# The low half of the attention weights moved from GpSimd to VectorE, and more tiles for the rows of x2

## The chip, the cores and the metric

The kernel runs on one core of a Trainium2 chip. The metric is device time in microseconds, the median of several executions. The engines are TensorE (PE, with its weight loads shown as PEld), VectorE (DVE), ScalarE (ACT), GpSimd (POOL) and SyncE (SP, which issues DMAs). Each engine takes its instructions strictly in the order in which they were written for it, and waits on semaphores for the other engines and for DMAs.

## The reference

Three stages follow one another: windowed attention with four sink keys, a dense layer with a maximum over three products, and an expert layer in which every token is assigned to one of eight experts under a capacity.

```python
def _attn_ref(q, k, v, n_sink, window):            # 4 x 8 heads, 768 x 64
    scores = scale * np.matmul(q, k.transpose(0, 1, 3, 2))
    keep = is_sink | in_window                      # 4 sinks, window 128
    scores = np.where(keep, scores, -1000000000.0)
    scores = scores - np.max(scores, axis=-1, keepdims=True)
    a = np.exp(scores)
    a = a / (np.sum(a, axis=-1, keepdims=True) + 1e-09)
    return np.matmul(a, v).astype(np.float32)

def _moe_ref(x, w1, w2, w3, w_out):                 # 3072 x 512, 768 wide
    h = np.maximum(np.maximum(x @ w1, x @ w2), x @ w3)
    return (h @ w_out).astype(np.float32)

def _moe2_ref(x, w_gate, w1, w2):                   # 8 experts, 384 tokens each
    logits = x @ w_gate
    ...                                             # tokens to experts, best first, cap 384
    for e in range(E):
        mask = assigned == e
        h = np.maximum(x[mask] @ w1[e], 0.0)
        out[mask] = h @ w2[e]
    return out.astype(np.float32)
```

## The kernel before, in words

Products that must be exact enough for the routing are computed with split operands: a value x is written as a high part (x rounded to the matmul's format, made by ScalarE) and a low part (x minus the high part, a subtraction), and three products (high-high, high-low, low-high) stand for one.

**Attention** works on 32 pairs of heads over half a sequence each, four pairs to a group, eight groups. For one pair, `load` fetches the operands, `prep` splits keys, queries and values (lines 101 to 116), `score` computes the masked scores, `soft` the softmax (its last multiplication, line 154, is GpSimd's), and `pv` multiplies with the values. In `pv`, for each of the two heads, TensorE transposes the weights (line 25), VectorE masks them into the tile A (line 170, 128x768), ScalarE makes the high part H (line 184), GpSimd the low part L (line 185), and TensorE multiplies H and L with the values (line 189, into po). ScalarE and VectorE then join the halves (lines 191, 192). Ten of the 32 pairs are taken without a split ("native", the first eight and two more); the remaining 22 pairs run lines 184 and 185 twice each, 44 in all.

**The dense layer** takes a group's four tiles x (split on line 28 and 29) and, for each of six row blocks f, makes three products into two alternating banks mm (line 290), takes their maximum (line 292 on ScalarE, 293 on VectorE, tile hm), and splits it (lines 298 and 299, tile HL). `x2` multiplies HL with the output weights (line 315), three row tiles t of two halves u; ScalarE copies each half from the bank to a row tile (line 317, `xo` or `xq`) and a DMA writes the row tile to the array x2d in DRAM (line 326). Group 0 is written to DRAM and multiplied later; groups 5 and 6 are multiplied later too, by `by_rows` and by `x2` with the pool `hp` (rows `xq`), together with group 7. `load_out` and `logits` use `xo` as well.

**The expert layer** ranks the tokens (VectorE with small TensorE counts, class `Route`), gathers the rows of x2d, and runs eight experts whose weights are streamed and split (lines 557 to 563).

All of attention and the dense layer stands in one block whose order is set by a planner when the program is built (`tc.block(schedule_with_timeline_sim=True)`): the attention of the next group is woven between the matmuls of the present one. Tiles of a pool are reused in turn (`bufs`); a reuse waits for the last reader of the buffer, a DMA included.

Of the kernel before, what the change touches and what calls it, by code (L numbers as in the profile page):

```python
# [19 lines left out]
FT=mybir.dt.float32; FR=mybir.dt.float32r; BF=mybir.dt.bfloat16; I32=mybir.dt.int32; U8=mybir.dt.uint8; U32=mybir.dt.uint32  # L20
AF=mybir.ActivationFunctionType; OP=mybir.AluOpType; AX=mybir.AxisListType
NEG=-8.0e9
def f32(ap): return ap.bitcast(FT)
def flip(nc,out,x,ident):
    nc.tensor.transpose(out,x,f32(ident))  # L25

def split(nc,hl,x):
    nc.scalar.activation(hl[0],x,AF.Copy)
    nc.vector.tensor_tensor(hl[1],x,f32(hl[0]),op=OP.subtract)

class Attn:
# [123 lines left out]
    def pv(s,u,x):  # L155
        nc=s.nc; w=s.w; T=u['T'].rearrange('p u j -> p (u j)'); hf=u['hf']; nb=u['nb']; nat=u['nat']
        psk=s.pst.tile([128,512],FT,name="pt")
        for i in range(3): flip(nc,psk[:,i*128:(i+1)*128],T[:,264*i+128:264*i+256],s.ident)
        PB=s.pb[u['n']%2]
        nc.scalar.activation(PB[0:8],psk[0:8,:384],AF.Copy)  # L160
        nc.vector.tensor_tensor(PB[32:40],psk[0:8,:384],f32(PB[0:8]),op=OP.subtract)
        jobs=[]
        if hf: jobs.append((0,128,0,0))
        for i in range(3): jobs.append((i*256+128,256 if i<2 else 128,i*128,i+hf))
        for h in range(2):
            pt=s.psp.tile([128,512],FT,name="pp")
            for i in range(3):
                flip(nc,pt[:,i*128:(i+1)*128],T[:,i*264+136*h:i*264+136*h+128],s.ident)
            A=s.two(dict(n=u['n']*2+h),[128,3,2,128],FT,"A")
            nc.vector.tensor_tensor(A,pt[:,:384].rearrange("p (i q) -> p i q",q=128)[:,:,None,:].to_broadcast([128,3,2,128]),  # L170
                s.ul[:,None,:,:].to_broadcast([128,3,2,128]),op=OP.mult)
            Af=A.rearrange("p i u q -> p (i u q)")
            a=slice(64*h,64*h+64); o=slice(64-64*h,128-64*h)
            if nat:
                if h==0:
                    po=s.psv.tile([128,512],FT,name="po")
                    for a_ in range(2): nc.tensor.matmul(po[:,:384],u['VK'][:,a_,:],PB,start=(a_==0),stop=False,skip_group_check=True)
                for c,n,q,blk in jobs:
                    nc.tensor.matmul(po[a,q:q+n],u['vn'][:,blk,h,:],Af[:,c:c+n],start=False,stop=True,skip_group_check=True)  # L179
                if h==1:  # L180
                    for c in x: split(nc,c,po[:,:384]) if type(c) is tuple else nc.scalar.activation(c,po[:,:384],AF.Copy)
                continue
            H=w.tile([128,768],FR,name="H"); L=w.tile([128,768],FR,name="L")
            nc.scalar.activation(H,Af,AF.Copy)  # L184
            nc.gpsimd.tensor_tensor(L,Af,f32(H),op=OP.subtract)  # L185
            po=s.psv.tile([128,512],FT,name="po")
            for part in (H,L):
                for j,(c,n,q,blk) in enumerate(jobs):
                    nc.tensor.matmul(po[:,q:q+n],u['VS'][:,blk,128*h:128*h+128],part[:,c:c+n],start=(part is H and j==0),stop=False,skip_group_check=True)  # L189
            nc.tensor.matmul(po[:,:384],u['VK'][:,h,:],PB,start=False,stop=True,skip_group_check=True)  # L190
            nc.scalar.activation(x[0][a,:],po[o,:384],AF.Copy)
            nc.vector.tensor_tensor(x[0][a,:],po[a,:384],x[0][a,:],op=OP.add)
# [18 lines left out]
class Moe1:  # L211
    def __init__(s, tc, words,wgate, consts, wpool, main, conv, mm, pt, pss, ident):
        s.tc=tc; s.nc=tc.nc; s.mm=mm; s.pss=pss; s.main=main; s.conv=conv; s.ident=ident; s.consts=consts
        s.src=words; s.wgate=wgate
        s.W=[[wpool.tile([128,4,768],FR,name=f"w{i}{x}") for x in "hl"] for i in range(3)]
        s.WO=None; s.at=None; s.stage=None; s.HL=None; s.n=0; s.loads=[]
        s.WG=main.tile([128,6,16],FR,name="wgt")
    def split(s,src,hi,lo):
        nc=s.nc
# [19 lines left out]
        return R.bitcast(FT)  # L239
    def pair(s,p):  # L240
        return tuple(s.main.tile([128,384],FR,name=f"x{x}{p}",bufs=1) for x in "hl")
    def part(s,x,f):
        return s.HL[:,"hl".index(x)*6+f]
    def load_w(s,f):
# [59 lines left out]
    def x2(s,H,t0,LG,x2d,n=260,pool=None,keep=None):  # L304

        nc=s.nc; main=s.main
        for t in range(3):
            o=pool.tile([128,512],FT,name="xq",bufs=3) if pool else main.tile([128,520],FT,name="xo",bufs=1)
            for u in range(2):
                c=slice(0,260) if n==260 else slice(4-4*u,260-4*u)  # L310
                ps=s.mm.tile([128,512],FT,name="mm")
                k=0
                for f in range(6):
                    for a,b in ((0,0),(0,1),(1,0)):
                        nc.tensor.matmul(ps[:,:n],H[f][a][:,t*128:(t+1)*128],s.WO[b][:,f,u,c],start=(k==0),stop=(k==17)); k+=1  # L315
                with s.tc.high_priority():
                    nc.scalar.activation(o[:,u*n:(u+1)*n],ps[:,0:n],AF.Copy)
                    if keep is not None:
                        for d in (2*u,2*u+1):
                            h,l=keep(t,d); c=ps[:,(d-2*u)*128:(d-2*u)*128+128]  # L320
                            nc.scalar.activation(h,c,AF.Copy)
                            nc.vector.tensor_tensor(l,c,f32(h),op=OP.subtract)
            if n==260:
                o,e=s.row(o,0)
                nc.scalar.activation(LG[:,t0+t,:].rearrange("p (u e) -> p u e",u=2),e,AF.Copy)
            nc.scalar.dma_start(x2d[(t0+t)*128:(t0+t+1)*128,:],o)
# [10 lines left out]
    def by_rows(s,spill,t0,x2d,accs,pool):  # L337

        nc=s.nc
        ps=[accs.tile([128,512],FT,name=f"acc{t}") for t in range(3)]  # L340
        for f in range(6):
            H=tuple(s.main.tile([128,384],FR,name=f"x{x}{f%4}",bufs=1) for x in "hl")
            for d,x in zip(spill[f],H): nc.sync.dma_start(f32(x),d)
            for t in range(3):
                for j,(a,b) in enumerate(((0,0),(0,1),(1,0))):
                    nc.tensor.matmul(ps[t],H[a][:,t*128:(t+1)*128],s.row(s.WO[b],f*520)[0],start=(f+j==0),stop=(f==5 and j==2))
        for t in range(3):
            o=pool.tile([128,512],FT,name="xq",bufs=3)
            with s.tc.high_priority(): nc.scalar.activation(o,ps[t],AF.Copy)
            nc.scalar.dma_start(x2d[(t0+t)*128:(t0+t+1)*128,:],o)  # L350
    def logits(s,H,t0,LG):
# [15 lines left out]
class Route:  # L367
# [4 lines left out]
    M=128  # L372
# [175 lines left out]
class Moe2:  # L548

    def __init__(s,tc,w1,w2,x2d,out,wpool,act,main,mm,acc,pt,ident,nring,part):  # L550
        s.tc=tc; s.nc=tc.nc; s.w1=w1; s.w2=w2; s.x2d=x2d; s.out=out
        s.wp=wpool; s.act=act; s.main=main; s.ng=0; s.mm=mm; s.acc=acc; s.pt=pt; s.ident=ident; s.nring=nring; s.part=part
        s.scat=[]; s.n=-1
# [80 lines left out]
def attention_mixtures(tc,q,k,v,vs,words,wg,u1,u2,out,off=60,spread=(0,1,3,4),native=8,order='a0 a0 a0 a0 w a1 w a1 w a1 w a1 w w a2',order1='a2 o o o o o o a2 a2',back=1,at=(1,0),s1=300,s2=400,nring=6):  # L634
    nc=tc.nc
    PS=bass.MemoryType.PSUM
    with ExitStack() as ctx:
        P=lambda n,b,**kw: ctx.enter_context(tc.tile_pool(name=n,bufs=b,**kw))
        A_=lambda n,b,**kw: tc.alloc_tile_pool(name=n,bufs=b,**kw)
# [5 lines left out]
        A=Attn(tc,q,k,v,vs,consts,ac,pst,psp,pss,psv,work)  # L645
        M=Moe1(tc,words,wg,consts,wpool,main,conv,mm,pst,pss,A.ident)
# [3 lines left out]
        def att(g,p):  # L650
            xs.setdefault(g,[])
            u=A.load(g//2,g%2,p,4*g+p<native or 4*g+p in (10,11)); A.prep(u); A.score(u); A.soft(u)
            x=main.tile([128,384],FT,name=f"x{p}") if g else M.pair(p)
            A.pv(u,[x]); xs[g].append(x)
        def lw(f): M.load_w(f)
        def lo(f): M.load_out(f)
        with tc.block(schedule_with_timeline_sim=True):
# [3 lines left out]
            def emit(o,p):  # L661
                n=cnt[o]=cnt.get(o,-1)+1
                if o[0]=='a':
                    if p:
                        with tc.high_priority(offset=off): att(int(o[1:]),n)
                    else: att(int(o[1:]),n)
                elif o=='w': lw(n)
                else:
                    A.extra=None; lo(n)
                    if n==5:  # L670
                        conv.release()
                        A.extra=A_("extra",1,side="right"); A.no=('A',)
                        A.ql.append(A.zeros([A.extra.tile([128,384],FR,name=f'ql{h}b') for h in range(2)]))
            for o in order.split():
                if o=='a2': A.behind=M.loads[-1]
# [2 lines left out]
            for g in range(NG):  # L678
# [15 lines left out]
                H6,H=H if g==NG-1 else None,M.group(xs[g],sp if g==0 else sp2 if g==NG-3 else None,hp if g==NG-1 else None,rest,between)  # L694
# [107 lines left out]
```

## Time and profile before

| what | us |
|---|---|
| median of 3 runs | 985.83 (981.25 to 990.14) |
| the profiled execution | 981.21 |
| its span, first to last instruction | 979.4 |
| TensorE busy in the span | 936.7 |
| VectorE busy | 693.3 |
| ScalarE busy | 486.2 |
| GpSimd busy | 340.9 |

The profiled execution stands at the low end of the runs. A busy share is an average over stages: attention with the dense layer takes up roughly the first 600 us, the routing and the experts the rest. A kernel line in a row (L185) is the line of the listing above. "Granted clock" is the share of TensorE's full clock (1.00 is 2.4 GHz, 0.50 is 1.2 GHz).

### The profile page before, as it was taken

The page shows a single profiled execution, that of the slowest core. Times are in us where ns is not written, and L with a number is a line of the kernel's source. Part 1 is how long each engine was busy: PE and PEld are TensorE (multiplying, and loading weights), DVE is VectorE, ACT ScalarE, POOL GpSimd, SP SyncE. Part 2 cuts the span into 40 slices and gives each one's busy share as a digit, 9 for nine tenths or more (in the row PEclk, how much of TensorE's full clock was granted, in tenths as well). Part 3 has the DMA queues.
Part 4 walks back from the last instruction along what each step waited for, and adds up shares of the span by engine and source line. Part 5 has one row for each costly group of instructions (what it writes and reads, how often), then busy time and mean ns, then how long its engine had stood idle before and what let it go on. Part 6 is the DMA issues. An engine that isn't in the chain of part 4 may idle for free.

```text
span 979.4 us, 18512 instructions
## 1 busy us (share of the span) xinstructions
PE 936.7 (96%) x6552; PEld 855.7 (87%) x6552; DVE 693.3 (71%) x1811; ACT 486.2 (50%) x1341; POOL 340.9 (35%) x315
## 2 busy tenths in 40 slices
PE   6899999999999999989999999999999999999996
PEld 4578899889999999979999898798888888888895
DVE  6778877687888877795655445889989879873320
ACT  4477553777576766666653211233433434344431
POOL 3687556136434634434343000011203122053331
PEclk8999999999999999999999999999999999999999
DMA  7464322341123122122110002634345353454420
GB/s 209 134 223 157 109 65 69 108 137 47 49 78 86 40 70 66 55 66 77 58 60 1 1 1 87 205 125 130 124 136 173 93 166 101 159 200 146 136 79 32
DMA packets 54444, 99.36 MB, mean 101 GB/s; under 512 B 7792, under 2 KB 24688, under 8 KB 54352
## 3 DMA queue, kind: packets, MB, share of 16 engines
q1 hardware_dynamic: 44464, 75.90, 25.3%
q0 software_dynamic: 3840, 12.45, 3.6%
q10 hardware_dynamic: 6048, 9.83, 2.7%
q8 instruction: 51, 0.84, 0.4%
q14 instruction: 41, 0.34, 0.1%
HBM read 82.17 MB, written 16.12 MB: 100 GB/s over the span
## 4 chain that ended last, share of the span: by engine, by line
PE 75%; DVE 9%; issue 5%; DMA 5%; ACT 4%; POOL 1%; SPq 1%; POOLq 0%; DVEq 0%; ACTq 0%
PE mm L290 27%; PE mm L618 11%; PE acc L611 11%; PE mm L315 7%; PE po L189 3%; PE rc L416 2%; PE po L179 2%; PE ps L130 2%; PE pt L25 2%; PE pp L25 2%; DMA sa<-in_u_dram 1%; DMA qf<-in_q_dram 1%; PE ps L132 1%; PE ps L133 1%; PE po L190 1%
## 5 line engine op out<-in xcount | busy, mean ns | idle before, releaser
L611 PE MATMUL acc<-wbh,HL 128*128 128x512 f32 x384 | 131.7, 399 | 0.0
L185 POOL TENSOR_TENSOR L<-A_w,H 128x768 fp32r<-128x768 f32 x42 | 80.2, 1909 | 100.7 <-ACT H L184 99.8
L630 POOL DMA_INDIRECT out_dram<-og,idx x24 | 32.2, 1344 | 182.4 <-ACT og L629 179.1
L315 PE MATMUL mm<-woh,HL 128*128 128x260 f32 (+1 forms) x432 | 91.9, 302 | 3.6 <-DVE HL L299 2.2
L293 DVE TENSOR_TENSOR hm<-mm,hm 128x384 f32<-128x384 f32 x96 | 53.2, 554 | 56.0 <-PE mm L290 47.8
L562 ACT ACTIVATE wah<-sa 128x512 fp32r<-128x512 f32 x64 | 40.5, 632 | 92.2 <-PE mm L618 73.0
L611 PEld LDWEIGHTS acc<-wbh,HL 128*128 128x128 f32 x384 | 71.9, 189 | 12.8
L315 PEld LDWEIGHTS mm<-woh,HL 128*128 128x128 f32 x432 | 73.1, 200 | 7.0 <-DVE HL L299 2.9
L562 ACT ACTIVATE wbh<-sb 128x512 fp32r<-128x512 f32 x64 | 40.4, 632 | 74.6 <-PE acc L611 71.9
L611 PE MATMUL acc<-wbl,HL 128*128 128x512 f32 x192 | 77.2, 402 | 0.0
L618 PE MATMUL mm<-HL,wah 128*128 128x384 f32 x256 | 68.8, 344 | 0.0
L290 PE MATMUL mm<-xh,w0h 128*128 128x384 f32 x192 | 66.7, 347 | 1.2 <-DVE hm L293 1.0
L290 PE MATMUL mm<-xh,w1h 128*128 128x384 f32 x192 | 66.2, 345 | 1.5 <-ACT hm L292 0.7
L290 PE MATMUL mm<-xh,w2h 128*128 128x384 f32 x192 | 66.6, 347 | 0.0
L563 DVE TENSOR_TENSOR wbl<-sb,wbh 128x512 fp32r<-128x512 f32 x64 | 43.9, 687 | 31.7 <-ACT wbh L562 31.7
L290 PE MATMUL mm<-xh,w0l 128*128 128x384 f32 x192 | 64.9, 338 | 0.4 <-POOL w0l L221 0.4
L290 PE MATMUL mm<-xl,w0h 128*128 128x384 f32 x192 | 64.9, 338 | 0.1
L290 PE MATMUL mm<-xh,w1l 128*128 128x384 f32 x192 | 64.9, 338 | 0.0
L290 PE MATMUL mm<-xl,w2h 128*128 128x384 f32 x192 | 64.9, 338 | 0.0
L290 PE MATMUL mm<-xh,w2l 128*128 128x384 f32 x192 | 64.8, 338 | 0.0
L290 PE MATMUL mm<-xl,w1h 128*128 128x384 f32 x192 | 64.6, 337 | 0.0
L622 DVE SCALAR_TENSOR_TENSOR HL<-mm,HL 128x384 fp32r<-128x384 f32 x64 | 35.4, 554 | 40.8 <-ACT HL L621 40.6
(331 smaller groups left out, 2843.9 us busy)
## 6 DMA issues: line engine op xcount, KB each, us to landing
sa<-in_u_dram SPq DMA_DIRECT2D x64, 256.0 KB
sb<-in_u_dram SPq DMA_DIRECT2D x64, 256.0 KB
HL<-in_words_dram SPq DMA_DIRECT2D x18, 512.0 KB
qn<-in_q_dram SPq DMA_DIRECT2D x88, 96.0 KB
x2d<-xo ACTq DMA_DIRECT2D x15, 256.0 KB
kn<-in_k_dram SPq DMA_DIRECT2D x12, 264.0 KB
st<-in_words_dram SPq DMA_DIRECT2D x6, 512.0 KB
vn<-in_v_dram SPq DMA_DIRECT2D x12, 256.0 KB
```

The costliest lines, as they stand in the source:

```text
L25: nc.tensor.transpose(out,x,f32(ident))
L185: nc.gpsimd.tensor_tensor(L,Af,f32(H),op=OP.subtract)
L189: nc.tensor.matmul(po[:,q:q+n],u['VS'][:,blk,128*h:128*h+128],part[:,c:c+n],start=(part is H and j==0),stop=False,skip_group_check=True)
L290: nc.tensor.matmul(ps[:,:384],s.W[i][a][:,p,f*128:(f+1)*128],X[p][b],start=(n==0),stop=(n==11)); n+=1
L293: else: nc.vector.tensor_tensor(m,ps[:,:384],m,op=OP.max)
L315: nc.tensor.matmul(ps[:,:n],H[f][a][:,t*128:(t+1)*128],s.WO[b][:,f,u,c],start=(k==0),stop=(k==17)); k+=1
L562: nc.scalar.activation(h,src,AF.Copy)
L563: (nc.gpsimd if s.n>=6 and nm=="wa" else nc.vector).tensor_tensor(l,src,f32(h),op=OP.subtract)
L611: s.mms.append(nc.tensor.matmul(acc[t],H[f][a][:,t*128:(t+1)*128],W[f][1][b],start=(f==0 and n==0),stop=(f==F-1 and n==2))); n+=1
L618: s.mms.append(nc.tensor.matmul(ps[:,:384],W[f][0][a][:,k,:],X[k][b],start=(n==0),stop=(n==11))); n+=1
L622: nc.vector.scalar_tensor_tensor(l,ps[:,:384],0.0,f32(h),op0=OP.max,op1=OP.subtract)
L630: st=nc.gpsimd.indirect_dma_start(out=s.out,out_offset=bass.IndirectOffsetOnAxis(ap=idx[:,t:t+1],axis=0),in_=o,in_offset=None)
```

## The change

The subtraction that makes L moves from GpSimd to VectorE (line 185 in both). `x2` takes its row tiles `xo` in turn from the pool `main` and from a second pool, `extra`, in which a tile of the same name and size is laid out; the row tiles `xq` have four buffers instead of three. The planner is run again on the new program. Lines after 241 move down by 3.

```diff
-            nc.gpsimd.tensor_tensor(L,Af,f32(H),op=OP.subtract)
+            nc.vector.tensor_tensor(L,Af,f32(H),op=OP.subtract)
...
-        s.WO=None; s.at=None; s.stage=None; s.HL=None; s.n=0; s.loads=[]
+        s.WO=None; s.at=None; s.stage=None; s.HL=None; s.nx=0; s.second=None; s.n=0; s.loads=[]
...
+    def room(s,t):
+        s.nx+=1
+        return s.main if s.nx%2 else s.second
...
-            o=pool.tile([128,512],FT,name="xq",bufs=3) if pool else main.tile([128,520],FT,name="xo",bufs=1)
+            o=pool.tile([128,512],FT,name="xq",bufs=4) if pool else s.room(t).tile([128,520],FT,name="xo",bufs=1)
...
-            o=pool.tile([128,512],FT,name="xq",bufs=3)
+            o=pool.tile([128,512],FT,name="xq",bufs=4)
...
-                        A.extra=A_("extra",1,side="right"); A.no=('A',)
+                        A.extra=M.second=A_("extra",1,side="right"); A.no=('A',)
```

On VectorE, the end of the dense layer of group 3: from the last maximum of the group (writes hm, L293) to the low part of its last block (writes HL, L299), which the first row tile of `x2` needs. Before:

```order
614 L293 TENSOR_TENSOR hm<-mm,hm 128x384
615 L29 TENSOR_TENSOR xl_5076<-x_4616,xh_5075 128x384
616 L192 TENSOR_TENSOR x_5158<-po,x_5158 64x384
617 L170 TENSOR_TENSOR A_w<-pp,ul 128x768
618 L29 TENSOR_TENSOR xl_5080<-x_4785,xh_5079 128x384
619 L104 TENSOR_TENSOR ql0b<-qn_6055,qs_6067 64x384
620 L142 COPY_PREDICATED T_w<-ca,ps 128x128
621 L102 TENSOR_TENSOR kh_x<-kn,kh_x 64x528
622 L104 TENSOR_TENSOR ql1b<-qn_6056,qs_6068 64x384
623 L142 COPY_PREDICATED T_w<-ca,ps 128x128
624 L102 TENSOR_TENSOR kh_x<-kn,kh_x 64x528
625 L299 TENSOR_TENSOR HL<-hm,HL 128x384
```

The same place on VectorE with the change (L296 is the old L293, L302 the old L299):

```order
664 L296 TENSOR_TENSOR hm<-mm,hm 128x384
665 L29 TENSOR_TENSOR xl_5076<-x_4616,xh_5075 128x384
666 L29 TENSOR_TENSOR xl_5080<-x_4785,xh_5079 128x384
667 L142 COPY_PREDICATED T_w<-ca,ps 128x128 x2
668 L192 TENSOR_TENSOR x_5158<-po,x_5158 64x384
669 L302 TENSOR_TENSOR HL<-hm,HL 128x384
```

Ten operations stood between the two; now five do. The splits of the next pair's queries and keys (L104, L102) have moved ahead of the last maximum.

On GpSimd, two pairs of the same stretch, before (T is the softmax tile, vk and vsp the split values):

```order
158 L154 TENSOR_TENSOR T_x<-T_x,l 128x792
159 L185 TENSOR_TENSOR L<-A_w,H 128x768
160 L108 CAST vk_103<-vns 40x2x64
161 L116 TENSOR_TENSOR vsp<-vn,vsp 128x4x128
162 L109 TENSOR_TENSOR vk_103<-vns,vk_103 40x128
163 L185 TENSOR_TENSOR L<-A_w,H 128x768
164 L154 TENSOR_TENSOR T_w<-T_w,l 128x792
165 L185 TENSOR_TENSOR L<-A_w,H 128x768
```

GpSimd's queue with the change, two pairs:

```order
133 L154 TENSOR_TENSOR T_x<-T_x,l 128x792
134 L108 CAST vk_103<-vns 40x2x64
135 L109 TENSOR_TENSOR vk_103<-vns,vk_103 40x128
136 L116 TENSOR_TENSOR vsp<-vn,vsp 128x3x128
137 L154 TENSOR_TENSOR T_w<-T_w,l 128x792 x2
```

The subtractions are gone from between the others; what is left in GpSimd's queue is one line 154, 108, 109 and 116 to a pair, and a memset in some.

## Rows read from the trace of the kernel before

**Rows 1.** The page, part 1: busy us, share of the span, instructions.

```profile
PE 936.7 (96%) x6552; PEld 855.7 (87%) x6552; DVE 693.3 (71%) x1811; ACT 486.2 (50%) x1341; POOL 340.9 (35%) x315
```

**Rows 2.** By stage: stretch, length, busy us of each engine, granted clock, DMA share, GB/s.

```profile
130.00:545.00 415.00, 403.04 (x2675) 390.72 (x2674) 302.12 (x580) 257.97 (x789) 180.48 (x156) 0.98 0.21 64
275.00:290.00 15.00, 13.45 (x94) 12.62 (x93) 13.62 (x28) 10.25 (x39) 3.96 (x4) 0.89 0.28 83
350.00:365.00 15.00, 13.29 (x94) 12.74 (x93) 11.49 (x22) 11.80 (x38) 6.11 (x6) 0.89 0.21 65
420.00:445.00 25.00, 20.32 (x131) 19.25 (x129) 19.69 (x34) 15.98 (x54) 8.96 (x7) 0.86 0.15 49
```

**Rows 3.** Timeline, 430 to 437 us: start, length, engine, line; in brackets idle before.

```profile
431.33 1.81 POOL L185 TENSOR_TENSOR L<-A_w,H 128x768 fp32r<-128x768 f32 x1
433.52 0.98 POOL L116 TENSOR_TENSOR vsp<-vn,vsp 128x384 fp32r<-128x384 f32 x1
...
431.25 3.67 DVE L104 TENSOR_TENSOR ql1b<-qn,qs 64x384 fp32r<-64x384 f32 x1
...
435.40 0.36 PE L132 MATMUL ps<-kh_w,qs 128*128 128x260 f32 x1 [3.80 <-DVE T_w L142]
...
436.63 0.80 PE L315 MATMUL mm<-woh,HL 128*128 128x260 f32 x2 [0.76 <-DVE HL L299]
```

**Rows 4.** Timeline around 272 to 282 and 350 to 360 us.

```profile
272.94 1.86 POOL L185 TENSOR_TENSOR L<-A_w,H 128x768 fp32r<-128x768 f32 x1 [3.30 <-ACT H L184]
273.08 2.15 DVE L102 TENSOR_TENSOR kh_x<-kn,kh_x 64x396 fp32r<-64x396 f32 x1
...
279.96 0.51 PE L315 MATMUL mm<-woh,HL 128*128 128x260 f32 x2 [0.56 <-DVE HL L299]
...
282.02 0.36 PE L132 MATMUL ps<-kh_x,qs 128*128 128x260 f32 x1 [0.84 <-DVE T_w L137]
...
350.62 1.86 POOL L185 TENSOR_TENSOR L<-A_w,H 128x768 fp32r<-128x768 f32 x1 [6.82 <-ACT H L184]
...
350.93 1.97 DVE L104 TENSOR_TENSOR ql<-qn,qs 64x384 fp32r<-64x384 f32 x1
...
358.02 0.51 PE L315 MATMUL mm<-woh,HL 128*128 128x260 f32 x2 [0.91 <-DVE HL L299]
359.32 0.67 PE L189 MATMUL po<-H,vsp 128*128 128x128 f32 x4 [0.80 <-DVE x L192]
```

**Rows 5.** Groups by line, 130 to 545 us: busy us, mean ns, idle before.

```profile
L185 POOL TENSOR_TENSOR L<-A_w,H 128x768 fp32r<-128x768 f32 x42 | 80.2, 1909 | 100.7 <-ACT H L184 99.8 <-PE pp L25 0.6
...
L170 DVE TENSOR_TENSOR A_w<-pp,ul 128x768 f32<-128x768 f32 x45 | 42.8, 951 | 9.8 <-PE pp L25 7.5 <-POOL L L185 2.0
...
L102 DVE TENSOR_TENSOR kh_x<-kn,kh_x 64x528 fp32r<-64x528 f32 (+1 forms) x20 | 20.8, 1041 | 3.0 <-ACT kh_x L101 2.3
...
L104 DVE TENSOR_TENSOR ql<-qn,qs 64x384 fp32r<-64x384 f32 x19 | 18.2, 958 | 1.2 <-ACT qs L103 0.9
...
L104 DVE TENSOR_TENSOR ql1b<-qn,qs 64x384 fp32r<-64x384 f32 x10 | 11.6, 1159 | 0.7 <-PE ps L133 0.4
```

**Rows 6.** Lines 104 and 102, whole run: count, shortest/median/longest ns.

```profile
L104 DVE TENSOR_TENSOR ql<-qn,qs x24: 542/556/2197, 101.1 to 450.0; 64x384 fp32r<-64x384 f32 x24
...
L102 DVE TENSOR_TENSOR kh_x<-kn,kh_x x20: 565/702/2594, 184.1 to 474.9; 64x528 fp32r<-64x528 f32 x12, 64x396 fp32r<-64x396 f32 x8
```

**Rows 7.** Waits, 130 to 545 us: who for whom, us in total, times, longest.

```profile
ACT xo L317 <- DMA x2d<-xo: 2.1, 1, 2.1
```

**Rows 8.** Timeline, 630 to 638 us, row tiles of the last groups.

```profile
630.90 0.33 ACTq L350 DMA_DIRECT2D x2d<-xq  x1
...
635.58 0.38 ACT L317 ACTIVATE xq<-mm 128x256 f32<-128x256 f32 x1 [3.22 <-DMA x2d<-xq]
...
637.63 0.58 PE L315 MATMUL mm<-woh,hh 128*128 128x256 f32 x1 [2.35 <-DVE HL L322]
```

**Rows 9.** The stretch 635 to 641 us, columns as in Rows 2.

```profile
635.00:641.00 6.00, 3.65 (x20) 3.44 (x19) 4.81 (x17) 4.54 (x12) 2.23 (x2) 0.72 0.58 168
```

## The prediction, made before the changed kernel was timed

> **What bounds the kernel now.** I began with the busy shares of the page [rows 1]. TensorE is busy for 936.7 of a span of 979.4 us, so only what makes it stop or run slowly can be won; 43 us of idle time is all there is, and much of it lies in the start and in the expert layer, which the change does not touch. Next I read the table by stage [rows 2]. The first line is the stretch in which the moved subtraction runs: 415 us long, TensorE busy 403.0. The reader should see two things in it: 12.0 us idle, and a granted clock of 0.98. The three short lines show where the clock goes: 0.89, 0.89 and 0.86 over 15, 15 and 25 us. Half speed (1.2 GHz) was granted for a few microseconds in each, right after TensorE had stood still several times. What that costs is (1 - 0.89) x 15 twice, 1.65 each, and 0.14 x 25 = 3.5, together 6.8 us of work. So TensorE loses 12.0 + 6.8 = **18.8 us** in this stage. That is the most the stage can give.
>
> Then the timeline at the largest stop, at 435 us [rows 3]. VectorE's subtraction of line 104 takes 3.67 us; such an operation takes 0.556 us in the median [rows 6]. It begins at 431.25. GpSimd's line 185 begins at 431.33, line 116 follows behind a short operation and ends at 434.50, and VectorE's ends at 434.92. An operation of VectorE that reads two tiles of SBUF is held up as long as GpSimd is in an unbroken run. TensorE waits 3.80 us for the copy queued behind it on VectorE and 0.76 us for HL. The same happens at 273 us and at 351 us [rows 4]: line 102 takes 2.15 us beside line 185 (shorter form undisturbed 0.565, [rows 6]), line 104 takes 1.97 us beside line 185, and some microseconds later, once VectorE's queue has become late, TensorE waits 0.56, 0.84, 0.91 and 0.80 us. In those two cases the link runs through a queue that was continuously busy, not through one wait. The six waits come to 7.7 us, and all three losses of clock lie there. Of the stage's 18.8 us, **14.5 us** hang on holds by line 185.
>
> The Trainium skill (SBUF — State Buffer, section "Who interferes with whom") says that a VectorE instruction with two SBUF inputs contends with a GpSimd instruction that reads SBUF, and that the second to issue blocks until the first finishes. The trace agrees on the blocking, but here the hold lasted through three GpSimd operations, not one.
>
> **The change, part by part.** *Line 185 leaves GpSimd.* 42 of its 44 operations take 80.2 us [rows 5], nearly half of the 180.5 us in which GpSimd is busy in the stage [rows 2]. How much VectorE is held: lines 104 and 102, 49 operations in three groups [rows 5], take 18.2 + 11.6 + 20.8 = 50.6 us, and undisturbed 29 x 0.556 + 20 x 0.702 at most = 30.2 us [rows 6]. So 20.4 us are holds, 0.42 us for each operation. With 47% of the holding work gone, about 9.6 us of these holds go.
>
> *It comes to VectorE.* 44 operations on 128x768. The nearest row is line 170, same shape and type, 0.951 us [rows 5]: 44 x 0.951 = 41.8 us. It reads one input from PSUM; the new one reads two from SBUF, so the undisturbed 0.556 us for half as many elements bounds it at 1.11 us from above. Being of the kind that is held, each also gets what is left of the holds, 0.42 x 0.53 = 0.22 us, 9.8 us together. VectorE's busy time in the stage goes from 302 to about 302 + 41.8 + 9.8 - 9.6 = 344 us of 415, from 73 to 83%. This lies beside TensorE's matmuls and costs nothing as such; the cover is that VectorE still idles 17% of the time. If it were gone, every microsecond of VectorE would be one of TensorE. Behind the new operation in VectorE's queue stands mostly the addition of line 192 or a maximum of line 293, and TensorE waits for those.
>
> *The order is written anew.* On VectorE the stretch that cost most now has five operations instead of ten between the last maximum and HL, with lines 104 and 102 ahead of it; a hold there is shorter and hits less. GpSimd's queue keeps lines 154, 108, 109 and 116, now side by side, so its unbroken runs without line 185 go on. Loads on SP's queue shift among themselves; none of TensorE's waits in rows 3 and 4 ends on a load, so they cost nothing.
>
> Together: of the 14.5 us I take two thirds as won, **9.7 us**, because about half of the holds stay and the queue is fuller. Bounds: all 18.8 us won; or as much again lost, 18.8 us, if the added 42 us makes as many new stops as the holds did.
>
> *A second tile for xo.* ScalarE waits for a row tile's DMA once, 2.1 us [rows 7], and a second bank of mm hides that from TensorE. Nothing; if the cover goes, 2.1 us.
>
> *A fourth tile for xq.* The row tiles go in turn: three for the x2 of group 6, three for by_rows, three for the x2 of group 7. With three buffers the last three reuse those whose DMAs had just been issued, at 630.90 and later. ScalarE stands 3.22 us until 635.58, its copy and splits are late, both banks of mm are full, and TensorE stops for 2.35 us [rows 8]. Then the clock falls: 0.72 over 6 us [rows 9], 0.28 x 6 = 1.7 us. With four buffers the first tile of group 7 takes one that was written out long before, and the second takes the one of 630.90 only two products of work later. The stop and the slow clock go: 2.35 + 1.7 = **4.0 us**. The expert layer behind it is TensorE's with routing on VectorE; the order there is the same as before, and the routing steps queued on VectorE behind the late split move forward too, so I take the whole. Bounds 0 and 4.0.
>
> **The sum.** 9.7 + 4.0 = 13.7 us less than the profiled execution's 981.2, so 967.5. That execution is the low end of the runs; the median shown is 985.8, 4.6 higher. What differs between executions are probably such stops, of which fewer are left, so I add half, 2.3: 969.8, rounded to **970 us**. Against 985.8 that is 1.6% less.
>
> **Rivals.** *Only the tail gives.* The planner spreads VectorE's new work, but the queue is fuller by ten points and each late operation meets a TensorE without reserve, so the stage loses its 18.8 us again. For it: half the holds stay. Against: the worst hold rested on line 185. Time 981.2 - 4.0 + 2.3 = 979.5.
>
> *Only the stage gives.* The row tile no longer stalls, but the routing of the second step or the gather of the rows sets the start of the experts, and TensorE stops there instead. Against it: routing was late for the same reason. Time 981.2 - 9.7 + 2.3 = 974.
>
> *Slower: VectorE's queue becomes what TensorE waits for.* The place is the pair of heads: mask (line 170), H on ScalarE, L on VectorE, then the products of L. Line 185 at the head of VectorE's queue waits for H if ScalarE is late, and the maximum of line 293 behind it waits too. GpSimd absorbed that: it stood idle 99.8 us for H [rows 5]. If one in three of the 44 stops TensorE as at 358 us, 0.91 us plus half the 1.65 us of a slow clock, that is 15 x 1.7 = 26 us new, against 14 won: 981.2 + 12 = 993. It decides once VectorE comes near 95% busy; 83% speaks against it.
>
> The Trainium skill (Perfetto Trace Analysis, section "Optimizing Scalar/DVE Operations") warns that moving work between GpSimd and VectorE may not help since they share a read port. By that the stage's gain would be nothing, which is the first rival's 979.5; the trace bears it out to the extent that half the holds remain.
>
> **How the numbers follow.** Forecast 0.57 (its own range 960 to 976), only the tail 0.23, only the stage 0.10, slower 0.10. The range reaches from 959 (all of 18.8 and 4.0 won is 958.4) to 983, which leaves out the slower case and the edges. About 1%, 10 us, is what a measurement can tell here from no change; 1% below the median is 976. Faster by over 1%: the forecast nearly always and some of the stage case, 0.60. Within 1%: the tail case and the rest, 0.31. Slower by over 1%: 0.09.
>
> **What would show it.** Line 185 stands on VectorE with a median near 0.95 us. The longest of lines 102 and 104 fall under 3 us and their means under 0.85. TensorE's busy time of the stage comes within 6 us of its length, with at most one stretch of half clock. ScalarE's wait for the xq DMA is gone, and so is the 2.35 us gap behind it. The prediction is wrong if TensorE's waits in the stage name line 185, or if the same 12 us idle stand at other places.

## The result and the profile after

| | median, us | runs |
|---|---|---|
| before | 987.81 | 981.25 to 990.14 (4) |
| changed | 975.24 | 973.18 to 976.00 (4) |
| ratio | 0.9889 | 95%: 0.9850 to 0.9929 |

The change makes the kernel 1.1% faster. The profiled execution took 973.18 us, 8.0 less than the one before. Of that, 12.7 us were won before the first expert, whose first product starts at 645.3 instead of 658.0, and 4.7 were given back among the experts.

**The stage.** The page's busy shares and the stretch of [rows 2] in the changed kernel (stretch, length, busy us of PE, PEld, DVE, ACT, POOL with their counts, granted clock, DMA share, GB/s):

```profile
PE 931.0 (96%) x6552; PEld 850.4 (88%) x6552; DVE 711.4 (73%) x1855; ACT 488.0 (50%) x1341; POOL 265.6 (27%) x271
```

```profile
130.00:545.00 415.00, 406.23 (x2725) 393.49 (x2724) 323.81 (x630) 262.15 (x796) 106.20 (x112) 1.00 0.21 64
```

TensorE idles 8.8 of the 415 us instead of 12.0, and the clock is 1.00 instead of 0.98: no stretch of half clock is left here. The clock gave more than the idle time did. A single short fall of the clock does not show in the two decimals over 415 us: in a second execution of the changed kernel (e4 below) the clock is 0.89 from 280 to 295 us, 1.7 us of work, and the long stretch reads 1.00 all the same. GpSimd fell from 180 to 106 us, VectorE rose from 302 to 324.

The rows of lines 185, 102 and 104, which answer to [rows 5] (busy us, mean ns, idle before), and below them whole-run rows that answer to [rows 6] (shortest/median/longest ns, first to last start):

```profile
L185 DVE TENSOR_TENSOR L<-A_w,H 128x768 fp32r<-128x768 f32 x42 | 43.8, 1044 | 16.4 <-ACT H L184 15.7
...
L102 DVE TENSOR_TENSOR kh_x<-kn,kh_x 64x528 fp32r<-64x528 f32 (+1 forms) x20 | 15.7, 785 | 2.2 <-ACT kh_x L101 1.6
L104 DVE TENSOR_TENSOR ql<-qn,qs 64x384 fp32r<-64x384 f32 x19 | 13.4, 704 | 1.0 <-ACT qs L103 0.6
...
L104 DVE TENSOR_TENSOR ql1b<-qn,qs 64x384 fp32r<-64x384 f32 x10 | 5.6, 555 | 0.9 <-ACT qs L103 0.6
...
L185 DVE TENSOR_TENSOR L<-wol,H 128x768 fp32r<-128x768 f32 x2 | 3.2, 1600 | 0.7 <-ACT H L184 0.7
```

```profile
L185 DVE TENSOR_TENSOR L<-A_w,H x42: 915/958/2176, 129.8 to 517.9; 128x768 fp32r<-128x768 f32 x42
```

```profile
L104 DVE TENSOR_TENSOR ql1b<-qn,qs x10: 555/555/556, 166.6 to 455.9; 64x384 fp32r<-64x384 f32 x10
```

The tile ql1b, which had the hold of 3.67 us [rows 3], is now not held once. Line 185 is itself held at times: median 0.958, longest 2.18 in this group. Its first and last start are a ruler for the stage that every kernel below has: they lie 517.9 - 129.8 = 388.1 us apart, against 399.5 before (from 130.8 to 530.3). The stretch between them, before and after:

```profile
130.80:530.30 399.50, 387.54 (x2580) 375.22 (x2579) 293.40 (x543) 253.84 (x782) 178.27 (x153) 0.98 0.22 66
```

```profile
129.80:517.90 388.10, 379.50 (x2568) 368.04 (x2567) 311.58 (x584) 254.99 (x781) 105.86 (x110) 1.00 0.23 68
```

The ruler ends at an instruction that is not TensorE's, and twelve products fewer lie within it now, so part of its 11.4 us is work that has moved behind its end. A second ruler, *dense*, goes by TensorE: from the first to the last start of the dense layer's products xh,w2l (before, then after):

```profile
L290 PE MATMUL mm<-xh,w2l x192: 332/337/440, 58.5 to 593.0; 128*128 128x384 f32 x192
```

```profile
L293 PE MATMUL mm<-xh,w2l x192: 333/337/441, 57.5 to 582.4; 128*128 128x384 f32 x192
```

That is 524.9 us instead of 534.5, 9.6 less. Behind it, before the tail, the first profile of the change gives 1.1 us back: 37.9 us from there to the tail's first product instead of 36.8, with a fall of the clock:

```profile
580.00:600.00 20.00, 18.51 (x199) 16.30 (x198) 10.84 (x54) 2.16 (x5) 1.87 (x4) 0.91 0.28 93
```

Holds are fewer, not gone. The longest that is left in the stage, in the timeline (start, length, engine, line):

```profile
426.71 1.50 POOL L154 TENSOR_TENSOR T_w<-T_w,l 128x792 f32<-128x792 f32 x1
426.84 3.30 DVE L102 TENSOR_TENSOR kh_w<-kn,kh_w 64x528 fp32r<-64x528 f32 x1
428.17 0.45 POOL L109 TENSOR_TENSOR vk<-vns,vk 40x128 fp32r<-40x128 f32 x1
428.59 0.99 POOL L116 TENSOR_TENSOR vsp<-vn,vsp 128x384 fp32r<-128x384 f32 x1
```

VectorE again waits out a run of three GpSimd operations, the last of which ends at 429.58; its own ends at 430.14. TensorE's largest waits in the stage are now for ScalarE's copies to xo:

```profile
PE mm L318 <- ACT xo L320: 3.8, 3, 1.6
```

**The tail.** The copy that stood 3.22 us for a row tile's DMA [rows 8] now waits 0.68 us, and for TensorE:

```profile
622.59 0.38 ACT L320 ACTIVATE xq<-mm 128x256 f32<-128x256 f32 x1 [0.68 <-PE mm L318]
```

The products of group 7's x2, from the first to the last (before, then after):

```profile
L315 PE MATMUL mm<-woh,hh x36: 275/282/582, 629.8 to 649.5; 128*128 128x256 f32 x36
```

```profile
L318 PE MATMUL mm<-woh,hh x36: 275/280/392, 620.3 to 636.9; 128*128 128x256 f32 x36
```

They take 16.6 us instead of 19.7.

**The experts.** From the first product with xh to the last with HL, the table by stretch of before, of the changed kernel, and of a second execution of the changed kernel (e4 below):

```profile
658.00:967.00 309.00, 306.08 (x2328) 267.93 (x2328) 220.85 (x745) 121.77 (x230) 73.05 (x58) 0.99 0.41 132
```

```profile
645.30:959.00 313.70, 306.74 (x2328) 267.70 (x2328) 220.99 (x745) 121.80 (x230) 72.10 (x58) 0.99 0.41 130
```

```profile
646.30:953.00 306.70, 304.72 (x2329) 266.83 (x2329) 220.79 (x745) 121.79 (x230) 73.03 (x58) 1.00 0.40 133
```

The same work takes 4.7 us more than before in the first profile of the change, and 2.3 less in the second. Idle time is 7.0 in the one and 2.0 in the other. The order there was not touched. The profile of before lost time there too, to a fall of the clock that no run below has:

```profile
795.00:805.00 10.00, 9.00 (x102) 7.97 (x102) 7.12 (x30) 1.64 (x3) 0.00 (x0) 0.83 0.23 67
```

The first of the stops, in the first profile of the change:

```profile
663.73 0.28 DVE L466 TENSOR_SCALAR_CACHE_REDUCE met<-rc,roomp 128x63 bf16<-128x63 f32 x1 [1.87 <-PE acc L614]
...
665.43 0.77 PE L419 MATMUL rc<-th,ohr 128*128 128x32 bf16 x24 [1.78 <-DVE th L414]
```

A routing step began late on VectorE, the next counting products stopped TensorE for 1.78 us, and the clock fell behind it:

```profile
665.00:670.00 5.00, 4.57 (x58) 3.95 (x59) 4.04 (x15) 1.01 (x2) 0.00 (x0) 0.67 0.38 111
```

So the 4.7 us belong to these two executions, not to the edit. Why the step began late is open.

### The profile page after: what moved, and what is told of

It is laid out like the page before. It is cut to its first block, busy times and chain, and to the rows that moved or that the text cites. A ratio compares the mean times of both kernels' runs of the same rounds, so it can differ in the third digit from the quotient of the medians.

```text
span 971.4 us, 18531 instructions
## 1 busy us (share of the span) xinstructions
PE 931.0 (96%) x6552; PEld 850.4 (88%) x6552; DVE 711.4 (73%) x1855; ACT 488.0 (50%) x1341; POOL 265.6 (27%) x271
## 4 chain that ended last, share of the span: by engine, by line
PE 72%; DVE 13%; issue 6%; ACT 3%; DMA 3%; POOL 1%; SPq 0%; POOLq 0%; DVEq 0%; ACTq 0%
PE mm L293 26%; PE mm L621 11%; PE acc L614 11%; PE mm L318 5%; PE rc L419 3%; PE po L189 3%; PE pt L25 2%; DVE kh_w L102 2%; PE po L179 2%; PE ps L130 1%; PE acc L349 1%; PE pp L25 1%; DVE L L185 1%; ACT T_w L151 1%; DMA HL<-in_words_dram 1%
## 5 line engine op out<-in xcount | busy, mean ns | idle before, releaser
L318 PE MATMUL mm<-woh,HL 128*128 128x260 f32 (+1 forms) x432 | 89.3, 293 | 4.9 <-ACT xo L320 3.8
L296 DVE TENSOR_TENSOR hm<-mm,hm 128x384 f32<-128x384 f32 x96 | 53.1, 553 | 51.9 <-PE mm L293 46.7
L318 PEld LDWEIGHTS mm<-woh,HL 128*128 128x128 f32 x432 | 70.3, 191 | 7.9 <-ACT xo L320 4.8
L293 PE MATMUL mm<-xh,w1h 128*128 128x384 f32 x192 | 66.9, 349 | 0.9 <-ACT hm L295 0.5
L293 PE MATMUL mm<-xh,w0h 128*128 128x384 f32 x192 | 66.5, 346 | 1.2 <-DVE hm L296 1.0
L293 PE MATMUL mm<-xh,w2h 128*128 128x384 f32 x192 | 66.4, 346 | 0.0
L625 DVE SCALAR_TENSOR_TENSOR HL<-mm,HL 128x384 fp32r<-128x384 f32 x64 | 35.5, 554 | 41.5 <-ACT HL L624 41.3
L293 PE MATMUL mm<-xh,w0l 128*128 128x384 f32 x192 | 65.1, 339 | 0.4 <-POOL w0l L221 0.4
L293 PE MATMUL mm<-xh,w2l 128*128 128x384 f32 x192 | 65.3, 340 | 0.0
L293 PE MATMUL mm<-xl,w2h 128*128 128x384 f32 x192 | 65.0, 338 | 0.0
L293 PE MATMUL mm<-xh,w1l 128*128 128x384 f32 x192 | 64.9, 338 | 0.0
L293 PE MATMUL mm<-xl,w0h 128*128 128x384 f32 x192 | 64.9, 338 | 0.0
L293 PE MATMUL mm<-xl,w1h 128*128 128x384 f32 x192 | 64.9, 338 | 0.0
L154 POOL TENSOR_TENSOR T_w<-T_w,l 128x792 f32<-128x792 f32 x22 | 34.2, 1554 | 105.4 <-DVE l L153 105.4
```

The costliest lines, as they stand in the source:

```text
L154: nc.gpsimd.tensor_tensor(T,T,l[:,:,None].to_broadcast([128,6,132]),op=OP.mult)
L293: nc.tensor.matmul(ps[:,:384],s.W[i][a][:,p,f*128:(f+1)*128],X[p][b],start=(n==0),stop=(n==11)); n+=1
L296: else: nc.vector.tensor_tensor(m,ps[:,:384],m,op=OP.max)
L625: nc.vector.scalar_tensor_tensor(l,ps[:,:384],0.0,f32(h),op0=OP.max,op1=OP.subtract)
```

## The experiments

Each kernel was timed beside the kernel before on its chip; ratios are to that. Four lengths are read from every trace: *stage*, first to last start of line 185; *dense*, first to last product xh,w2l; *tail*, first to last product woh,hh of x2; *experts*, first product xh to last product HL.

| kernel | stage | dense | tail | experts | median, before | ratio (95%) |
|---|---|---|---|---|---|---|
| before | 399.5 | 534.5 | 19.7 | 309.0 | | |
| changed | 388.1 | 524.9 | 16.6 | 313.7 | 975.24, 987.81 | 0.9889 (0.9850 to 0.9929) |
| e1, line 185 alone | 386.6 | 523.4 | 20.1 | 307.4 | 969.26, 979.41 | 0.9908 (0.9882 to 0.9934) |
| e2, xq alone | 398.7 | 534.0 | 16.8 | 306.7 | 975.73, 979.41 | 0.9953 (0.9935 to 0.9971) |
| e3, second pool alone | 391.4 | 527.4 | 20.9 | 306.6 | 976.93, 979.41 | 0.9978 (0.9955 to 1.0000) |
| e8, line 185 and xq | 386.5 | 524.1 | 15.4 | 306.9 | 963.94, 979.41 | 0.9846 (0.9823 to 0.9870) |
| e4, the change again | 387.9 | 525.4 | 15.8 | 306.7 | 966.55, 978.38 | 0.9885 (0.9863 to 0.9907) |
| e5, as e8, again | 386.4 | 523.5 | 16.0 | 307.1 | 967.73, 978.38 | 0.9897 (0.9870 to 0.9924) |
| e6, reading twin | 400.3 | 536.6 | 15.6 | 306.6 | 977.46, 978.38 | 0.9994 (0.9980 to 1.0008) |
| e7, writing twin | 389.8 | 526.8 | 16.0 | 306.8 | 972.64, 978.38 | 0.9945 (0.9922 to 0.9968) |
| e9, line 154 to VectorE | 397.1 | 534.5 | 16.6 | 307.3 | 977.56, 977.22 | 0.9989 (0.9964 to 1.0013) |
| e10, line 154 to ScalarE | 384.9 | 519.6 | 16.9 | 307.8 | 970.16, 977.22 | 0.9921 (0.9895 to 0.9947) |
| e11, e10 and line 116 | 395.6 | 532.0 | 16.0 | 307.5 | 978.46, 977.22 | 1.0005 (0.9986 to 1.0024) |

The lengths are of one execution each, the medians of 4 to 12 (of the kernel before, up to 22). The planner writes a new order for each kernel, so a kernel differs from another by more than its edit.

**e1: line 185 alone.**

```diff
-            nc.gpsimd.tensor_tensor(L,Af,f32(H),op=OP.subtract)
+            nc.vector.tensor_tensor(L,Af,f32(H),op=OP.subtract)
```

> Line 185 on VectorE alone; row tiles as before. Theory A (the holds were what cost): the stage up to the last product of line 290 is shorter by about 10 us as in the whole change, the wait for the xq DMA at the end of the dense layer stays, and the time is 0.988 to 0.993 of before. Theory B (the row tiles and the newly written order made the gain, the holds did not): 0.997 or more.

0.9908: the moved subtraction alone gives about 10 us, with the tail as long as before.

```profile
130.00:545.00 415.00, 405.35 (x2733) 394.02 (x2732) 317.52 (x632) 262.92 (x798) 103.16 (x112) 1.00 0.21 64
```

TensorE idles 9.7 us and the clock is 1.00: nearly the changed kernel's stage.

**e2: the fourth xq tile alone.**

```diff
-            o=pool.tile([128,512],FT,name="xq",bufs=3) if pool else main.tile([128,520],FT,name="xo",bufs=1)
+            o=pool.tile([128,512],FT,name="xq",bufs=4) if pool else main.tile([128,520],FT,name="xo",bufs=1)
...
-            o=pool.tile([128,512],FT,name="xq",bufs=3)
+            o=pool.tile([128,512],FT,name="xq",bufs=4)
```

> Four buffers for xq alone, line 185 on GpSimd. Theory A: the 3.2 us wait of ScalarE and the 2.35 us stop of TensorE behind it are gone, the first product of the experts comes 3 to 4 us earlier, and the expert layer keeps it only in part: 0.996 to 0.999 of before. Theory B: 0.993 or less. If the experts' pace is set by something that does not depend on when they start, the start is earlier and the end is not: 1.000.

0.9953, which is 3.7 us, a little more gain than the 0.996 to 0.999 expected; the tail is 2.9 shorter, the stage within a microsecond of before, and the experts lose nothing of it. The term is right.

**e3: the second pool for xo alone.** Against the changed kernel:

```diff
-            nc.vector.tensor_tensor(L,Af,f32(H),op=OP.subtract)
+            nc.gpsimd.tensor_tensor(L,Af,f32(H),op=OP.subtract)
...
-            o=pool.tile([128,512],FT,name="xq",bufs=4)
+            o=pool.tile([128,512],FT,name="xq",bufs=3)
```

> The second tile for xo alone, line 185 on GpSimd, xq with three buffers. Theory A: TensorE hardly waited for xo before (two waits of 0.1 us), so 0.998 to 1.002. Rival: TensorE's waits for the copies into xo, 3.8 us in the changed kernel, come from the second tile, which lets the row tiles follow one another more closely than ScalarE serves them: 1.002 to 1.005.

```profile
130.00:545.00 415.00, 403.02 (x2717) 392.87 (x2716) 301.35 (x585) 261.32 (x799) 181.33 (x156) 1.00 0.21 65
```

The ratio reaches 1.0 at the edge of its interval. But this execution's stage is 391.4 us, and its dense layer 7.1 us shorter than before: the idle time is the 12.0 of before, and of the lost clock one fall is left, again hidden in the 1.00:

```profile
350.00:365.00 15.00, 11.79 (x86) 11.22 (x85) 11.79 (x21) 10.10 (x34) 6.38 (x5) 0.89 0.27 82
```

A new order with GpSimd's work unchanged can thus save 5.1 of the clock's 6.8 us in one execution; over 12 runs it is worth 2.5 us. Against e1's 10.2 the intervals do not overlap.

**e8: line 185 and xq, without the second pool.** Against the kernel before, e1's and e2's edits together:

```diff
+            nc.vector.tensor_tensor(L,Af,f32(H),op=OP.subtract)
...
+            o=pool.tile([128,512],FT,name="xq",bufs=4) if pool else main.tile([128,520],FT,name="xo",bufs=1)
```

> The change without the second tile for xo. Theory A: as the whole change, 0.987 to 0.991 of before. Rival (the second tile costs 3.8 us of waits): 0.984 to 0.986, and TensorE's waits for the copies into xo fall under 1 us.

963.94, the lowest of all, and 15.5 us under before on its chip: e1's 10.2 and e2's 3.7 make 13.8 (unrounded). The two add up within the intervals. The ratio lies in the range of the rival, not in that of theory A, and TensorE's waits for the copies into xo are 1.0 us, as the rival had it; so e4 and e5 repeat the pair.

**e4 and e5: the change and the same kernel as e8, side by side on another chip.**

> The changed kernel unaltered, beside the same without the second tile for xo. If the two stops of 1.8 and 1.7 us at the start of the experts and the slow clock behind the first belong to that one execution, they are absent here and the ratio is 0.985 to 0.988; if they belong to the change, they return at the same places and the ratio stays 0.988 to 0.991.

> The change without the second tile for xo, once more. If the second tile costs what the waits for the copies into xo show (3.8 us against 1.0), this is 0.002 to 0.004 under the changed kernel on the same chip; if it costs nothing, within 0.002 of it.

0.9885 and 0.9897: no difference. The lead of e8 is not repeated, so the second xo tile is worth nothing that these runs resolve. For e4 the two signs part: the stops among the experts are absent, but the ratio lies in the range that was to go with their return; it is the trace that places them. The waits of TensorE for the copies into xo are there again, though: 3.8 us in e4's trace, and in e5's

```profile
PE mm L315 <- ACT xo L317: 0.9, 3, 0.4
```

ScalarE's own wait for the DMA of xo stands in the changed kernel too, 1.8 us against 2.1 in [rows 7]:

```profile
ACT xo L320 <- DMA x2d<-xo: 1.8, 1, 1.8
```

**e6: the reading twin.** The changed kernel, with four GpSimd subtractions of 128x160 behind line 185 that read its two operands into an unused tile.

```diff
             nc.vector.tensor_tensor(L,Af,f32(H),op=OP.subtract)
+            for z in range(4): nc.gpsimd.tensor_tensor(w.tile([128,160],FT,name="tw",bufs=1),Af[:,z*160:z*160+160],f32(H)[:,z*160:z*160+160],op=OP.subtract)
```

> The changed kernel, and GpSimd again does a subtraction of the same two tiles at the same point, in four pieces of 160 columns, into a tile that nobody reads: its load is as before the change, VectorE's stays as after. Theory A (holds by GpSimd's reads are what cost): VectorE's operations of lines 101 to 104 and 185 are held again, 15 us or more beyond the changed kernel, and 6 to 15 us of the gain are lost: 0.995 to 1.003 of before. Theory C (the gain came from the shorter way from H to L and the new order, not from the holds): within 0.003 of the changed kernel.

```profile
130.00:545.00 415.00, 398.16 (x2666) 384.67 (x2665) 330.21 (x597) 261.11 (x796) 227.39 (x287) 1.00 0.21 65
```

```profile
L185 DVE TENSOR_TENSOR L<-A_w,H 128x768 fp32r<-128x768 f32 x42 | 50.4, 1201 | 13.2 <-ACT H L184 10.6 <-PE po L190 1.5 <-PE ps L133 0.6
```

```profile
391.19 1.94 POOL L186 TENSOR_TENSOR tw<-A_w,H 128x160 f32<-128x160 f32 x3
391.81 0.93 DVE L303 TENSOR_TENSOR HL<-hm,HL 128x384 fp32r<-128x384 f32 x1 [0.59 <-ACT HL L302]
```

The whole gain is gone: stage 400.3, 0.9994. Nobody waits for the twins' result. TensorE idles 16.8 us, with one fall of the clock (0.83 from 280 to 290 us), and line 185 on VectorE rises to 1.20 us. The last two rows show one hold: 0.93 us beside a twin, median 0.559.

The twins are no plain return of what was moved, however. They keep GpSimd busy for 123.8 us, not 80.2, and they have a second effect: VectorE's line 170 waits until a twin has read the tile A that it is to write again.

```profile
L186 POOL TENSOR_TENSOR tw<-A_w,H 128x160 f32<-128x160 f32 x168 | 123.8, 737 | 82.5 <-ACT H L184 74.5
```

```profile
DVE A_w L170 <- POOL tw L186: 10.1, 13, 1.9
```

Before the change 2.0 us of such waiting stood there [rows 5], after it none. And the holds are fewer than expected. The stage of e6 by its own ruler has as many VectorE operations as the changed kernel's, which take 10.7 us longer:

```profile
133.60:533.90 400.30, 383.46 (x2573) 370.01 (x2573) 322.25 (x584) 254.49 (x781) 223.81 (x282) 1.00 0.22 66
```

The three groups of lines 104 and 102 take 15.5 + 6.4 + 15.4 = 37.3 us against 34.7 with the change; most of the rest is line 185. So e6 shows that reads by GpSimd can cost the whole gain, not how much of that is holds and how much the wait for A.

**e7: the writing twin.** Eight memsets of the same tile in place of the subtractions, started by the same H.

```diff
+            for z in range(8):
+                ms=nc.gpsimd.memset(w.tile([128,160],FT,name="tw",bufs=1),0.0)
...
```

> The same place and about the same time on GpSimd (eight memsets of 160 columns, some 1.8 us), but only writing. Theory A, as far as only GpSimd operations that read SBUF hold VectorE: no longer holds than in the changed kernel, time within 0.003 of it. Rival (any GpSimd work beside VectorE holds it up): as with the reading twin.

```profile
130.00:545.00 415.00, 403.78 (x2719) 393.63 (x2718) 317.06 (x631) 263.37 (x798) 182.75 (x464) 1.00 0.21 64
```

```profile
L185 DVE TENSOR_TENSOR L<-A_w,H 128x768 fp32r<-128x768 f32 x42 | 41.4, 986 | 11.4 <-ACT H L184 10.7
```

```profile
249.51 1.10 POOL L187 MEMSET tw<- 128x160 f32 x4
249.96 0.95 DVE L185 TENSOR_TENSOR L<-A_w,H 128x768 fp32r<-128x768 f32 x1
```

GpSimd is as busy as before the change (183 us), but VectorE is not held: 0.95 us beside the memsets, mean 0.986, and line 170 does not wait for them. Neither effect of e6 is here. The stage of this execution is 389.8. The median of seven runs is 972.64, though, where a time within 0.003 of the change was expected: half the gain is missing, and the profiled run is the fastest of the seven (968.11 to 974.19). On the holds the run is clear; on the time it is not, and what costs the other half is open.

**e9, e10, e11: more of GpSimd's work moved, on top of e8.** Line 154 (the softmax's last multiplication) to VectorE; to ScalarE, as six operations; and with that line 116 (the values' low part) to VectorE.

```diff
-        nc.gpsimd.tensor_tensor(T,T,l[:,:,None].to_broadcast([128,6,132]),op=OP.mult)
+        nc.vector.tensor_tensor(T,T,l[:,:,None].to_broadcast([128,6,132]),op=OP.mult)
```

```diff
+        for j in range(6): nc.scalar.activation(T[:,j,:],T[:,j,:],AF.Copy,scale=l[:,j:j+1])
```

```diff
-            nc.gpsimd.tensor_tensor(lo,u['vn'][:,:nb],f32(hi),op=OP.subtract)
+            nc.vector.tensor_tensor(lo,u['vn'][:,:nb],f32(hi),op=OP.subtract)
```

> The change without the second tile for xo, and the softmax's last multiplication (line 154) on VectorE too: 32 operations of about 0.97 us more on VectorE, GpSimd's longest reading operation gone. Theory A: the holds by line 154 (the largest that are left) go, but VectorE comes to about 340 of 405 us in the stage; holds won and load added nearly even out, 0.985 to 0.990 of before. Rival (only holds count): 0.980 to 0.984. Rival (VectorE's load is the limit now): 0.992 or more.

> The same with the multiplication on ScalarE as six scaled copies of 132 columns for each pair, about 1.6 us of ScalarE for 1.5 us of GpSimd. ScalarE is the least busy of the three that count (263 of 405 us). Theory A: the holds by line 154 go at no cost to VectorE, 0.980 to 0.986 of before. Rival: ScalarE's queue is late instead (it makes H and copies every bank), 0.990 or more.

> As the one before, and the low half of the values (line 116, 22 operations) on VectorE, so that of GpSimd's reading operations only the small ones of lines 108 and 109 and those of the weights stay. Theory A: VectorE's holds fall under 12 us, its load rises by 15 us: 0.978 to 0.986. Rival (load is the limit): slower than the one before by 0.003 or more.

The stage of e9, e10 and e11, in this order:

```profile
130.00:545.00 415.00, 404.56 (x2715) 394.13 (x2714) 327.64 (x657) 267.61 (x810) 66.08 (x91) 0.99 0.22 67
```

```profile
130.00:545.00 415.00, 408.89 (x2771) 398.98 (x2769) 313.70 (x642) 309.05 (x955) 70.67 (x91) 1.00 0.22 66
```

```profile
130.00:545.00 415.00, 404.78 (x2721) 393.61 (x2720) 317.19 (x640) 307.26 (x956) 45.95 (x73) 0.99 0.23 68
```

All three lose ahead of the stage. The dense layer's first product starts at 41.3 us in e9, 42.2 in e10 and 41.7 in e11, against 35.0 to 37.1 in every kernel that leaves line 154 on GpSimd. In e8 and in e9:

```profile
L290 PE MATMUL mm<-xh,w0h x192: 333/337/532, 35.9 to 577.6; 128*128 128x384 f32 x192
```

```profile
L290 PE MATMUL mm<-xh,w0h x192: 332/337/531, 41.3 to 591.8; 128*128 128x384 f32 x192
```

That is 5 to 6 us of what they lack against e8. Behind it e10 has the shortest stage of all, 384.9 us with 6.1 idle. e9 and e11 lose nearly the whole gain of the stage as well, dense 534.5 and 532.0: TensorE idles 10.4 and 10.2 us of the 415, little more than in e8 (9.5), but the clock falls again, in e9 to 0.89 from 205 to 220 and from 290 to 305 us and to 0.83 from 370 to 380, in e11 at the first and the last of these. Among TensorE's waits are steps that are late in VectorE's queue. The largest in e9, and then in e11:

```profile
208.80 0.33 PE L25 MATMUL pp<-ident,T_x 128*128 128x128 f32 x1 [2.05 <-DVE A_w L170]
```

```profile
444.02 0.39 PE L189 MATMUL po<-H,vsp 128*128 128x256 f32 x1 [1.96 <-DVE x L192]
```

In e11 line 185 is hardly held any more, 0.961 us in the mean, yet e11 is the slowest; VectorE now stands 11.6 us at that line for TensorE's products:

```profile
L185 DVE TENSOR_TENSOR L<-A_w,H 128x768 fp32r<-128x768 f32 x42 | 40.4, 961 | 29.7 <-ACT H L184 17.8 <-PE po L189 11.6
```

So in these orders taking reads off GpSimd stops paying when VectorE gets the next piece. The times of e9 and e11 came out in the range of the rival that had VectorE's load as the limit, but not by busy time: that is 328 us of 415 in e9 and 317 in e11, against 324 in the change. e10's 0.9921 lies in the range of a late ScalarE, though its stage is the shortest. Each of the three is one order of the planner's, and ScalarE is fuller in e11 too (307 us), so that VectorE's queue is the reason is likely, not shown.

## Why the prediction came out right, and where it was off

**The bound** was read rightly: TensorE's stops in one stage, the slow clock behind them, and one stop in the tail. All of e1, e2 and e8 gain at these two places.

**The stage, 9.7 us forecast:** by the dense ruler 9.6 in the first profile, 9.1 in e4, 11.1 in e1; by line 185's, 11.4, 11.6 and 12.9. The size came out, its make-up did not. "Two thirds of 14.5" took the stops and the clock alike: the clock's 6.8 us came back whole (5.1 of them in e4), while idle time fell by only 3.2 us in the same 415 (3.6 in e4). I had thought of stops as what is won, with the clock as their follower; the clock was the larger part. That the two together make two thirds is luck.

**Holds by GpSimd** as the cause: e6 puts reads back and loses everything, e7 puts writes back and VectorE is not held. Shown for the holds. That holds make the time is not shown to the end: e6's twins hold VectorE for 10.7 us and keep its line 170 waiting for another 10.1, e7's median lost half the gain, and e3's order saved most of the lost clock in one execution without touching GpSimd. The Trainium skill (SBUF — State Buffer, section "Who interferes with whom") separates GpSimd instructions that read from those that only write, and e6 and e7 agree: 1.20 us against 0.99 for line 185.

**VectorE's load, 344 us forecast:** 324. Line 185 took 43.8 + 3.2 = 47.0 us instead of 51.6, near enough. The holds fell further than by 47%: the three groups that I summed went from 50.6 to 15.7 + 13.4 + 5.6 = 34.7 us, by 15.9 and not 9.6. The other 9.4 us, by 302.1 + 47.0 - 323.8 = 25.3, fell on operations that I had not counted as held at all.

**The marks.** Line 185's median, the means under 0.85 us of the groups that I named, no half clock in the stage, and the quiet tail came as said. Two did not: a hold of 3.30 us stayed (line 102, tile kh_w; ahead of the stage, at 95 us, one of 4.53 us stands in both kernels), and TensorE idles 8.8 us, not 6. Its idle time moved to the copies of xo in part (3.8 us). One sign of being wrong came, though small: TensorE waits for line 185 once, for 0.3 us.

```profile
PE po L189 <- DVE L L185: 0.3, 1, 0.3
```

**The tail, 4.0 us:** 3.1 in the first profile, 3.9 in e4, 4.3 in e8. Right, though 2.9 in e2.

**xo, nothing:** nothing measurable (e4 and e5), and ScalarE's wait stayed.

**The sum, 13.7 off a profiled execution:** 12.7 - 4.7 = 8.0 in the first profile; 14.0 in e4, whose span is 965.4 against 979.4. Of e4's 14.0, dense and tail make 9.1 + 3.9 = 13.0; 2.3 more come from the experts, where the profile of before had lost time to its clock, and 1.3 are lost at the start. So the close hit of 13.7 is in part luck. By medians the change gives 12.6 us on the first chip and 978.38 - 966.55 = 11.8 on the other. The forecast of 970 lies 5.2 below the median: the profiled execution was to take 967.5 and took 973.2, most of that the 4.7 among the experts. The 2.3 that I added from it to the median measured 2.1.

**The rivals.** The time alone does not decide: 975.24 is nearer to the 974 of *only the stage gives* than to 970. That rival fell with e2 and with the experts' start, 12.7 us earlier in the first profile; *only the tail gives* fell with e1. That moving work between GpSimd and VectorE may not help (the Trainium skill, Perfetto Trace Analysis, section "Optimizing Scalar/DVE Operations") was behind the tail rival. The first piece helped all the same, 0.9908; a further one did not, 0.9989 in e9. *Slower through VectorE's queue* did not come, but its point of decision, near 95% busy, finds no support: e9 and e11 lost the gain at 76 to 79%.

## What to carry to other kernels

Where one engine's reads hold up another's operations, count the excess of these over their undisturbed time, line by line, before moving anything; here moving one line took 22% of GpSimd's busy time and shortened VectorE's other operations in the stage by 25 us. Look for the slow clock behind each stop, but do not take it as a fixed price: the stage before lost 6.8 us of clock with 12.0 idle, e6 about 1.7 with 16.8. And watch TensorE's waits when you move more: the mean busy share of the receiving engine did not tell where it stopped paying. A twin that puts work back must be read for its side effects, as e6's wait for A shows.

## What the hardware showed beyond that

- The longest holds in the stage lasted through an unbroken run of GpSimd's reading operations, 3.67 us before and 3.30 after, each across three of them. 128x160 pieces hold too, though 123.8 us of them (e6) made VectorE's operations only 10.7 us longer.
- The same instructions of the expert layer took 306.7 us in one execution and 313.7 in another, with 2.0 and 7.0 us of TensorE's idle time, most of it behind routing steps, and a stretch of slow clock in the second. One execution of each kernel would have told 4.7 us of this as the change's.
